# Attention and two mixture layers on one core: k and q in one transfer, half weight tiles side by side in HBM, logits split by half rows

## The chip, the cores and the metric

The kernel runs on one core of one Trainium2 chip. The metric is device time in microseconds, from the first to the last instruction with what lies around them, of one execution of the program. Times are medians over runs; profiles are of one execution.

## What is computed

```python
def _attn_ref(q, k, v):                     # q, k, v: (4, 8, 576, 64) float32
    scores = scale * np.matmul(q, k.transpose(0, 1, 3, 2))
    mask_local = (rel >= 0) & (rel < 32)                        # heads 0 to 3
    mask_strided = (rel >= 0) & (pos[None, :] % 32 == pos[:, None] % 32)   # heads 4 to 7
    ...                                     # softmax over the allowed positions
    return np.matmul(attn, v)

def _moe_ref(x, phi, w1, w2):               # x: (2304, 512); soft mixture, 8 experts, 4 slots each
    logits = x @ phi                        # (2304, 32)
    d = softmax(logits, axis=0); slot_input = d.T @ x
    for e in range(8):
        slot_out[e] = relu(slot_input[e] @ w1[e]) @ w2[e]       # 512 -> 1024 -> 512
    return softmax(logits, axis=1) @ slot_out

def _moe2_ref(x, w_gate, w_val, w_out):     # gated MLP, 512 -> 1536 -> 512
    return (silu(x @ w_gate) * (x @ w_val)) @ w_out
```

A local head attends to the last 32 positions; a strided head attends to every 32nd position before its own. The gate, value and output weights of the last layer come as float64 and are converted on the chip; the rest is float32.

## The kernel before

**Attention.** There are 16 units; a unit is one head of a pair of batches (`bp`), its 64 dimensions of the first batch on partitions 0 to 63 and of the second on 64 to 127. Within each batch pair the order of heads is 0, 1, 4, 5, 2, 3, 6, 7, so units 2, 3, 6, 7, 10, 11, 14, 15 are strided (`y` is 1). For strided heads the host reorders the 576 positions (t, r), t being 0 to 17 and r 0 to 31, so that those with equal r lie together; they are in the order (r, t). A strided head is then local too: both kinds work on nine tiles of 64 positions with a window of 96 keys (local) or 80 keys (strided).

For each unit, `load_qk` brings q and k (one transfer each, 128 rows of 2304 bytes) into one of three buffers, and `load_v` brings v (64 rows of 4680 bytes) into partitions 32 to 95 (local) or 16 to 79 (strided) of one of two buffers; three POOL copies (L261) then repeat the overlap between windows on the partitions below. `qk` makes the scores (L285), with scale, mask and maximum on DVE (L289, L290); `expo` the exponentials on ACT (L295); `tr` transposes on PE (L303) with copies on ACT (L304); `pv` multiplies with v (L320) and divides on DVE.

**The loop** (L590 to L619) runs steps n = 0 to 18, as an order written out by hand. In step n come `qk(n)`, `load_qk(n+3)`, `tr(n-1)`, `expo(n, 0)`, side work, `expo(n, 1)`, `pv(n-1)`, `load_v(n+1)`, and two half weight tiles (`load_half`); then further side work. All these transfers are issued by SP, on one queue, in that order.

**Logits.** Two heads give one tile of x, with 128 features. After each pair of heads `xtr` transposes that tile on PE (L338), ACT copies it (L339), and `logits` (L358) adds its product with phi to the logits of the batch pair in one PSUM bank. The 576 columns of each batch are split over the partitions: `hf` is the half (288 columns), `b` the batch, and the four (hf, b) lie on four groups of 32 partitions. The logits are kept in the plain order of positions (t, r), and half 0 is t from 0 to 8. A local head's x is read in order. A strided head's x is in order (r, t), so it is read with a step of 18 elements and written in order. There are eight such calls, four of them strided, the last two in steps 14 and 17. Then `tok_max`, `tok_exp` (exponentials into `e2`), `e_perm` (the same in order (r, t), on partitions 64 to 127), and `tok_end` (logits into `Lb`); `etr` and `slot` (L423) form the slot inputs.

**Weights.** 32 tiles of expert weights (1 MB each, 16 of w1, 16 of w2) and three tiles of the last layer come as half tiles of 512 KB, 70 in all, in the order of the list `loads`. In HBM a tile is 128 rows of 8192 bytes, and a half takes 4096 bytes out of each row. Fifteen buffers plus three for the tiles of the last layer hold 36 halves during the attention. The other 34 go to memory that the attention frees; the first of these takes a tile of the tag `x`, which is free when the slot matmuls of the first batch pair (`slot(0, 1)`, step 18) have read it. After the expert weights SP issues the first four whole tiles (1 MB) of the remaining weights of the last layer with `load_g` (L656), and the others when a buffer comes free.

**Last stage.** From about 160 us the gated MLP runs on PE (L794, L795, L821), with conversion of weights on ACT and DVE beside it. It is the larger part of the time.

Of the kernel before, what the change touches and what calls it, by code (L numbers as in the profile page):

```python
# [9 lines left out]
F32 = mybir.dt.float32  # L10
F32R = mybir.dt.float32r
I32 = mybir.dt.int32
BF16 = mybir.dt.bfloat16
AF = mybir.ActivationFunctionType
# [3 lines left out]
S = 576  # L18
HD = 64
NT = 9  # L20
PAD = 32
# [20 lines left out]
NQK = 3  # L42
# [29 lines left out]
def bits(a):  # L72
    return a.view(np.int64)
# [12 lines left out]

def layout(q, k, v, moe_phi, moe_w1, moe_w2, moe2_w_gate, moe2_w_val, moe2_w_out):
    pi = perm_index()
    qh = np.empty((16, 2, HD, S), np.float32)
    kh = np.empty((16, 2, HD, S), np.float32)  # L90
    vw = np.ones((16, 64, 2, NT, HD + 1), np.float32)
    for u, (bp, h) in enumerate(UNITS):
        y = h // 4
        o = pi if y else np.arange(S)
        qh[u] = q[2 * bp:2 * bp + 2, h][:, o].transpose(0, 2, 1)
        kh[u] = k[2 * bp:2 * bp + 2, h][:, o].transpose(0, 2, 1)
        vw[u, ..., :HD] = v[2 * bp:2 * bp + 2, h][:, o].reshape(2, NT, 64, HD).transpose(2, 0, 1, 3)
    w1 = moe_w1.reshape(8, 4, 128, 2, 512).transpose(0, 3, 2, 1, 4).reshape(16, 128, 2048)
    w2 = moe_w2.reshape(8, 2, 4, 128, 512).transpose(0, 1, 3, 2, 4).reshape(16, 128, 2048)
    g = bits(moe2_w_gate).reshape(4, 128, 12, 128)  # L100
    a = bits(moe2_w_val).reshape(4, 128, 12, 128)
    wgv = np.stack([g, a], axis=3).transpose(2, 1, 0, 3, 4).reshape(12, 128, 1024)
    wo = bits(moe2_w_out).reshape(6, 2, 128, 512).transpose(0, 2, 1, 3).reshape(6, 128, 1024)
    phi = moe_phi.reshape(4, 128, 32).transpose(1, 0, 2).reshape(128, 128)
    arrs = dict(cst=constants(), phi=phi, qh=qh.reshape(16, 128, S), kh=kh.reshape(16, 128, S),
                vh=vw.reshape(16, 64, -1),
                w1=w1, w2=w2, wgv=wgv, wo=wo)
    return {n: np.ascontiguousarray(x) for n, x in arrs.items()}


@with_exitstack
def build(ctx: ExitStack, tc: tile.TileContext, cst, phi, qh, kh, vh, w1, w2, wgv, wo, out):
    nc = tc.nc
    PE, ACT, DVE, POOL, SP = nc.tensor, nc.scalar, nc.vector, nc.gpsimd, nc.sync

# [8 lines left out]
    lp = es_ld.enter_context(tc.tile_pool(name="ld", bufs=1, side="right"))  # L124
# [11 lines left out]
    Lb = cp.tile([128, S], F32, name="Lb")  # L136
# [2 lines left out]

    qbd, kt, vt = [], [], []  # L140
    for j in range(NQK):
        qbd.append(lp.tile([128, S], F32, name=f"q{j}"))
        kt.append(lp.tile([128, PAD + S], F32, name=f"k{j}"))
    for j in range(NV):
        vt.append(lp.tile([96, 2 * NT * (HD + 1)], F32, name=f"v{j}"))
    col = lp.tile([128, 128], F32, name="col")
# [14 lines left out]
    def load_half(k, pool=wp, bufs=NB):  # L161
        for _ in range(k):
            if wn[0] >= NW:
                return
            j, hf = loads[wn[0]]
            if j in SPEC:
                wt[j, hf] = (ap_.tile([128, 1024], F32, tag="xT", name="wx", bufs=1) if hf and j == SPEC[0] else
                             ap_.tile([128, 1024], F32, tag="x", name="wx", bufs=6))
            elif j == SPLIT:
                wt[j, hf] = ap_.tile([128, 1024], F32, tag="eT", name="wx", bufs=1) if hf else tmp[:, 0:1024]  # L170
            elif hf == 0:
                a = pool.tile([128, 2048], F32, tag="w", name="w", bufs=bufs)
                if j in PRE:
                    gt[j] = a.bitcast(I32)
                wt[j, 0], wt[j, 1] = a[:, 0:1024], a[:, 1024:2048]
            if j in PRE:
                o, i = wt[j, hf].bitcast(I32), (wgv if j[0] == "g" else wo)[j[1]][:, 512 * hf:512 * hf + 512].bitcast(I32)
            else:
                o, i = wt[j, hf], wsrc[j][:, 1024 * hf:1024 * hf + 1024]
            SP.dma_start(out=o, in_=i)  # L180
            wn[0] += 1

# [64 lines left out]
    def load_qk(u):  # L247
        if u >= 16:
            return
        SP.dma_start(out=qbd[u % NQK], in_=qh[u])  # L250
        SP.dma_start(out=kt[u % NQK][:, PAD:], in_=kh[u])

    def load_v(u):
        if u >= 16:
# [89 lines left out]
    def logits(bp, y, st):  # L344
        first, last = (y, st) == (0, 0), (y, st) == (1, 1)
        if first:
            lg[bp] = bank("lg", 1)
        a = xT.pop((bp, y, st))
        for hf in range(2):
            for b in range(2):  # L350
                o = 64 * hf + 32 * b
                if y:
                    rhs = a[:, b, :].rearrange("p (r t) -> p t r", t=18)[:, 9 * hf:9 * hf + 9, :]
                    dst = lg[bp][o:o + 32, 0:288].rearrange("p (t r) -> p t r", r=32)
                else:
                    rhs = a[:, b, 288 * hf:288 * hf + 288]
                    dst = lg[bp][o:o + 32, 0:288]
                PE.matmul(out=dst, lhsT=phi_t[:, 2 * y + st, :], rhs=rhs, start=first, stop=last,  # L358
                          skip_group_check=True)

# [11 lines left out]
    def tok_exp(bp):  # L372
        mh = nmx[bp]
        e2[bp] = ap_.tile([128, S], F32, tag="e2", name="e2", bufs=1)
        s2 = ap_.tile([64, 2], F32, tag="s2", name="s2", bufs=2)
        for hf in range(2):
            h = slice(64 * hf, 64 * hf + 64)
            ACT.activation(out=e2[bp][0:64, 288 * hf:288 * hf + 288], in_=lg[bp][h, 0:288], func=AF.Exp,
                           bias=mh[h, 2:3], scale=1.0, accum_out=s2[:, hf:hf + 1])
        nmx[bp] = mh, s2  # L380

    def e_perm(bp):
        for hf in range(2):
            DVE.tensor_copy(e2[bp][64:128].rearrange("p (r t) -> p r t", t=18)[:, :, 9 * hf:9 * hf + 9],
                            e2[bp][0:64].rearrange("p (t r) -> p r t", r=32)[:, :, 9 * hf:9 * hf + 9])

    def tok_end(bp):
        r = slice(64 * bp, 64 * bp + 64)
        mh, s2 = nmx[bp]
        DVE.tensor_scalar_mul(m_sb[r], mh[0:64, 2:3], -1.0)  # L390
        DVE.tensor_tensor(out=s_sb[:, bp:bp + 1], in0=s2[:, 0:1], in1=s2[:, 1:2], op=ALU.add)
        DVE.tensor_copy(Lb[r, 0:288], lg[bp][0:64, 0:288])
        DVE.tensor_copy(Lb[r, 288:576], lg[bp][64:128, 0:288])

    eT = ap_.tile([128, NT, 2, 2, 32], F32, tag="eT", name="eT", bufs=1)
    WIN = (((0, 4), (4, 8), (8, 10)), WIN1)
# [98 lines left out]
    with tc.manual_schedule():  # L495
# [155 lines left out]
        def load_g(pool, tag, bufs):  # L651
            if gn[0] < len(gsrc):
                kind, j = gsrc[gn[0]]
                t = pool.tile([128, 2048], F32, tag=tag, name=tag, bufs=bufs)
                gt[kind, j] = t.bitcast(I32)
                SP.dma_start(out=gt[kind, j], in_=(wgv if kind == "g" else wo)[j].bitcast(I32))  # L656
                gn[0] += 1

        def c_soft(q):
# [301 lines left out]
                stage(n)  # L961


_NAMES = ['cst', 'phi', 'qh', 'kh', 'vh', 'w1', 'w2', 'wgv', 'wo']


# [15 lines left out]
```

## Time and profile before

| | us |
|---|---|
| median of 3 runs | 368.44 |
| lowest and highest run | 367.56 and 370.82 |
| the profiled execution | 367.68 |
| its span, from the first to the last instruction | 365.9 |
| PE busy | 341.4 |
| DVE busy | 233.2 |
| ACT busy | 193.9 |
| POOL busy | 139.3 |

The profile has the engines PE (matmul), PEld (weight load of PE), DVE, ACT and POOL, and the DMA queue issued by SP (SPq). Times in its rows are microseconds from the start of the span. The DMA share is the mean busy share of the core's 16 DMA engines. Matmuls are pipelined and their ends are modelled, so PE that is busy is not PE at its peak; a matmul in 32-bit floats shows as two instructions. An arrow names what ended an engine's idle time.

### The profile page before, as it was taken

The numbers are of one execution on the slowest core, as the hardware profiler recorded it, in microseconds if no ns is written. First come the engines' busy times: TensorE is split into PE (matmuls) and PEld (weight loads), VectorE is DVE, ScalarE is ACT, GpSimd is POOL, SyncE is SP. The second block draws the span as 40 slices with busy tenths as digits, with TensorE's granted clock in tenths as the row PEclk, the third lists the DMA queues.
The fourth block names the chain that finished last, engine by engine and source line by source line (L and its number), as shares of the span: only waits on it lengthen the run. The fifth ranks groups of instructions, "written<-read, shape, count | busy, mean of one in ns | idle before, by whom it ended". The sixth has DMA issues, their size and how long they took to land.

```text
span 365.9 us, 7445 instructions
## 1 busy us (share of the span) xinstructions
PE 341.4 (93%) x2860; PEld 249.3 (68%) x2860; DVE 233.2 (64%) x487; ACT 193.9 (53%) x462; POOL 139.3 (38%) x147
## 2 busy tenths in 40 slices
PE   8869999899879999979999999999998999999995
PEld 4758677788657333246786668677685788888885
DVE  4957858867744026276987998999787924241442
ACT  2966977787631004146775656556456445344441
POOL 2213222122110020024848497356459564444431
PEclk9989999899999999996999999999999999999999
DMA  7999999998849999982042444333300003030321
GB/s 256 384 298 382 316 315 383 286 372 282 291 151 381 402 407 407 419 338 116 1 134 97 127 186 147 115 116 116 115 0 3 1 0 117 0 115 2 116 104 69
DMA packets 21188, 71.94 MB, mean 197 GB/s; under 512 B 2592, under 2 KB 2976, under 8 KB 19232
## 3 DMA queue, kind: packets, MB, share of 16 engines
q1 hardware_dynamic: 21008, 71.45, 54.8%
q8 instruction: 23, 0.38, 0.4%
q14 instruction: 13, 0.11, 0.1%
q10 hardware_dynamic: 144, 0.01, 0.0%
HBM read 66.73 MB, written 4.72 MB: 195 GB/s over the span
## 4 chain that ended last, share of the span: by engine, by line
PE 59%; DMA 18%; DVE 8%; ACT 5%; POOL 4%; issue 4%; SPq 1%; DVEq 0%; POOLq 0%; ACTq 0%
PE o L821 31%; DMA v<-in_vh 7%; DMA w<-in_w 5%; PE pv L320 4%; PE sc L285 4%; PE tr L303 3%; PE gv L794 3%; DMA g<-in_wgv 3%; DMA wx<-in_w 3%; PE gv L795 3%; PE tr L338 2%; DVE h L801 2%; PE lg L358 2%; PE gv L774 2%; PE sc L626 1%
## 5 line engine op out<-in xcount | busy, mean ns | idle before, releaser
L803 POOL TENSOR_TENSOR hl<-h,hh 128x512 fp32r<-128x512 f32 (+1 forms) x60 | 72.4, 1208 | 90.7 <-ACT hh L802 90.5
L821 PE MATMUL o<-woh,hh 128*128 128x512 f32 (+1 forms) x222 | 86.7, 392 | 0.2 <-DVE acc L846 0.2
L821 PE MATMUL o<-wol,hh 128*128 128x512 f32 (+1 forms) x222 | 86.0, 389 | 0.0
L801 DVE TENSOR_TENSOR h<-gv,sg 128x512 f32<-128x512 f32 (+1 forms) x59 | 37.5, 636 | 55.8 <-ACT sg L800 42.5
L821 PE MATMUL o<-woh,hl 128*128 128x512 f32 (+1 forms) x222 | 66.8, 390 | 0.6 <-POOL hl L803 0.4
L802 ACT CAST hh<-h 128x512 fp32r<-128x512 f32 (+1 forms) x60 | 34.7, 578 | 54.7 <-DVE h L801 54.7
L261 POOL COPY v<-v 32x390 f32<-32x390 f32 (+3 forms) x48 | 22.2, 494 | 71.8 <-DMA v<-in_vh 60.6
L821 PEld LDWEIGHTS o<-woh,hh 128*128 128x128 f32 x222 | 42.2, 190 | 10.0 <-DVE acc L846 0.7
L821 PEld LDWEIGHTS o<-woh,hl 128*128 128x128 f32 x222 | 41.8, 190 | 10.4 <-POOL hl L803 1.9
L821 PEld LDWEIGHTS o<-wol,hh 128*128 128x128 f32 x222 | 42.3, 190 | 8.6
L800 ACT ACTIVATE sg<-gv 128x512 f32<-128x512 f32 (+1 forms) x60 | 33.5, 558 | 20.1 <-PE gv L794 19.3
L295 ACT ACTIVATE tmp<-tmp,mx 128x96 f32<-128x96 f32 (+1 forms) x144 | 39.0, 358 | 8.3 <-DVE mx L290 8.3
L320 PEld LDWEIGHTS pv<-v,tmp 96*64 96x64 f32 (+1 forms) x576 | 20.6, 140 | 13.5 <-ACT tmp L295 7.0
L320 PE MATMUL pv<-v,tmp 96*64 96x65 f32 (+1 forms) x576 | 23.9, 231 | 5.9 <-ACT tmp L295 3.1
L285 PE MATMUL sc<-k,q 64*64 64x96 f32 (+1 forms) x576 | 26.4, 245 | 1.7 <-DVE mx L290 1.1
L794 PE MATMUL gv<-cs,St 128*128 128x512 f32 (+1 forms) x60 | 25.6, 426 | 1.9 <-DVE St L783 1.9
L304 ACT COPY tmp<-tr 96x384 f32<-96x384 f32 (+1 forms) x48 | 19.7, 479 | 12.9 <-PE tr L303 12.9
L285 PEld LDWEIGHTS sc<-k,q 64*64 64x64 f32 x576 | 23.7, 138 | 4.1 <-DVE mx L290 1.2
L765 POOL TENSOR_TENSOR wol<-wo,woh 128x512 fp32r<-128x512 f32 x12 | 15.4, 1299 | 24.0 <-DMA g<-in_wgv 24.0
L795 PE MATMUL gv<-cs,St 128*128 128x512 f32 (+1 forms) x59 | 22.4, 379 | 0.2 <-DVE h L801 0.2
L219 DVE SCALAR_TENSOR_TENSOR cv<-g,cv 128x512 int32<-128x512 int32 x30 | 20.8, 692 | 0.6
L303 PE MATMUL tr<-cst_t,tmp 128*96 128x128 f32 (+1 forms) x144 | 19.4, 278 | 1.5 <-ACT xT L339 1.5
(160 smaller groups left out, 486.5 us busy)
## 6 DMA issues: line engine op xcount, KB each, us to landing
w<-in_w SPq DMA_DIRECT2D x56, 512.0 KB, 9.9
g<-in_wgv SPq DMA_DIRECT2D x10, 1024.0 KB, 4.8
g<-in_wo SPq DMA_DIRECT2D x5, 1024.0 KB, 4.8
v<-in_vh SPq DMA_DIRECT2D x16, 292.5 KB, 7.9
q<-in_qh SPq DMA_DIRECT2D x16, 288.0 KB, 9.3
k<-in_kh SPq DMA_DIRECT2D x16, 288.0 KB, 9.0
out<-osb SPq DMA_DIRECT2D x17, 256.0 KB, 2.0
wx<-in_w SPq DMA_DIRECT2D x7, 512.0 KB, 10.9
```

The costliest lines, as they stand in the source:

```text
L261: POOL.tensor_copy(t4[0:W - 64, :, i0:i1, :], t4[64:W, :, i0 - 1:i1 - 1, :])
L285: PE.matmul(out=ps[h, W * (i - i0):W * (i - i0) + W], lhsT=q[h, 64 * i:64 * i + 64], rhs=k[h, c0:c0 + W], start=True, stop=True, skip_grou ...
L295: ACT.activation(out=e[:, i], in_=e[:, i], func=AF.Exp, scale=1.0, bias=mx[:, i:i + 1])
L303: PE.transpose(ps[0:W, 128 * j:128 * j + 128], e[:, 3 * t + j], ident)
L320: PE.matmul(out=ps[64 * b:64 * b + 64, 65 * (i - i0):65 * (i - i0) + 65], lhsT=attile[0:W, i, 64 * b:64 * b + 64], rhs=v[0:W, 65 * (NT * b ...
L794: PE.matmul(out=pg[:, 0:n], lhsT=St[f][:, 0:128], rhs=csf[:, t0:t0 + n], start=True, stop=True)
L795: PE.matmul(out=pvv[:, 0:n], lhsT=St[f][:, 128:256], rhs=csf[:, t0:t0 + n], start=True, stop=True)
L800: ACT.activation(out=sg[:, 0:n], in_=pg[:, 0:n], func=AF.Silu)
L801: DVE.tensor_tensor(out=h[:, 0:n], in0=pvv[:, 0:n], in1=sg[:, 0:n], op=ALU.mult)
L802: ACT.copy(hh[bi, f][:, 0:n], h[:, 0:n])
L803: POOL.tensor_tensor(out=hl[bi, f][:, 0:n], in0=h[:, 0:n], in1=hh[bi, f][:, 0:n].bitcast(F32), op=ALU.subtract)
L821: PE.matmul(out=o[:, 0:c], lhsT=(a, a, l)[i][:, 128 * t:128 * t + 128], rhs=(woh, wol, woh)[i][f][:, c * k:c * k + c], start=(first and i ...
```

## The change

The host puts k and q of a unit into one array `kq`, k first, and `load_qk` brings both in one transfer into one buffer, in which q now lies behind k. The host stores expert weights and the last layer's weights by half tiles, so that a half tile is one piece of 512 KB; whole tiles (`load_g`) are then read as two rows of 4096 bytes for each partition. The logits are split over the partitions by r rather than by t: half 0 is r from 0 to 15. A strided head's x is then read in order and written to PSUM with a step of 16 elements; a local head's x is read in runs of 16 elements and written in order. `tok_exp`, `e_perm` and `tok_end` follow that split.

```diff
-    qh = np.empty((16, 2, HD, S), np.float32)
-    kh = np.empty((16, 2, HD, S), np.float32)
+    kq = np.empty((16, 2, HD, 2, S), np.float32)
...
-        qh[u] = q[2 * bp:2 * bp + 2, h][:, o].transpose(0, 2, 1)
-        kh[u] = k[2 * bp:2 * bp + 2, h][:, o].transpose(0, 2, 1)
+        kq[u, :, :, 0] = k[2 * bp:2 * bp + 2, h][:, o].transpose(0, 2, 1)
+        kq[u, :, :, 1] = q[2 * bp:2 * bp + 2, h][:, o].transpose(0, 2, 1)
...
+    w1, w2 = (a.reshape(16, 128, 2, 1024).transpose(0, 2, 1, 3) for a in (w1, w2))
+    wgv, wo = (a.reshape(-1, 128, 2, 512).transpose(0, 2, 1, 3) for a in (wgv, wo))
...
-        qbd.append(lp.tile([128, S], F32, name=f"q{j}"))
-        kt.append(lp.tile([128, PAD + S], F32, name=f"k{j}"))
+        a = lp.tile([128, PAD + 2 * S], F32, name=f"k{j}")
+        kt.append(a)
+        qbd.append(a[:, PAD + S:])
...
-                o, i = wt[j, hf].bitcast(I32), (wgv if j[0] == "g" else wo)[j[1]][:, 512 * hf:512 * hf + 512].bitcast(I32)
+                o, i = wt[j, hf].bitcast(I32), (wgv if j[0] == "g" else wo)[j[1], hf].bitcast(I32)
             else:
-                o, i = wt[j, hf], wsrc[j][:, 1024 * hf:1024 * hf + 1024]
+                o, i = wt[j, hf], wsrc[j][hf]
...
-        SP.dma_start(out=qbd[u % NQK], in_=qh[u])
-        SP.dma_start(out=kt[u % NQK][:, PAD:], in_=kh[u])
+        SP.dma_start(out=kt[u % NQK][:, PAD:], in_=kq[u])
...
                 o = 64 * hf + 32 * b
+                dst = lg[bp][o:o + 32, 0:288]
                 if y:
-                    rhs = a[:, b, :].rearrange("p (r t) -> p t r", t=18)[:, 9 * hf:9 * hf + 9, :]
-                    dst = lg[bp][o:o + 32, 0:288].rearrange("p (t r) -> p t r", r=32)
+                    rhs = a[:, b, 288 * hf:288 * hf + 288]
+                    dst = dst.rearrange("p (t r) -> p r t", r=16)
                 else:
-                    rhs = a[:, b, 288 * hf:288 * hf + 288]
-                    dst = lg[bp][o:o + 32, 0:288]
+                    rhs = a[:, b, :].rearrange("p (t r) -> p t r", r=32)[:, :, 16 * hf:16 * hf + 16]
+                    dst = dst.rearrange("p (t r) -> p t r", r=16)
...
-            ACT.activation(out=e2[bp][0:64, 288 * hf:288 * hf + 288], in_=lg[bp][h, 0:288], func=AF.Exp,
+            ACT.activation(out=e2[bp][0:64].rearrange("p (t r) -> p t r", r=32)[:, :, 16 * hf:16 * hf + 16],
+                           in_=lg[bp][h, 0:288].rearrange("p (t r) -> p t r", r=16), func=AF.Exp,
...
-            DVE.tensor_copy(e2[bp][64:128].rearrange("p (r t) -> p r t", t=18)[:, :, 9 * hf:9 * hf + 9],
-                            e2[bp][0:64].rearrange("p (t r) -> p r t", r=32)[:, :, 9 * hf:9 * hf + 9])
+            DVE.tensor_copy(e2[bp][64:128, 288 * hf:288 * hf + 288].rearrange("p (r t) -> p r t", t=18),
+                            e2[bp][0:64].rearrange("p (t r) -> p r t", r=32)[:, 16 * hf:16 * hf + 16])
...
-        DVE.tensor_copy(Lb[r, 0:288], lg[bp][0:64, 0:288])
-        DVE.tensor_copy(Lb[r, 288:576], lg[bp][64:128, 0:288])
+        for hf in range(2):
+            DVE.tensor_copy(Lb[r].rearrange("p (t r) -> p t r", r=32)[:, :, 16 * hf:16 * hf + 16],
+                            lg[bp][64 * hf:64 * hf + 64, 0:288].rearrange("p (t r) -> p t r", r=16))
...
-                SP.dma_start(out=gt[kind, j], in_=(wgv if kind == "g" else wo)[j].bitcast(I32))
+                SP.dma_start(out=gt[kind, j].rearrange("p (h c) -> p h c", h=2),
+                             in_=(wgv if kind == "g" else wo)[j].rearrange("h p c -> p h c").bitcast(I32))
```

## Rows read from the trace of the kernel before

**Rows 1.** Stretches: length, busy us of each engine, granted PE clock, DMA share, GB/s

```profile
2.00:4.00 2.00, 2.00 (x6) 0.64 (x5) 0.10 (x1) 0.45 (x1) 0.00 (x0) 1.00 0.85 287
4.00:6.00 2.00, 2.00 (x20) 1.05 (x20) 1.23 (x5) 0.00 (x0) 0.09 (x1) 1.00 0.93 305
...
24.00:30.00 6.00, 6.00 (x70) 5.29 (x74) 3.97 (x11) 2.06 (x5) 0.81 (x3) 0.72 1.02 282
30.00:39.40 9.40, 9.40 (x177) 7.86 (x173) 7.80 (x20) 8.00 (x27) 3.26 (x7) 1.00 1.04 408
39.40:46.50 7.10, 6.39 (x113) 4.50 (x114) 4.94 (x13) 6.22 (x21) 2.05 (x5) 1.00 1.04 291
46.50:53.00 6.50, 6.02 (x98) 4.69 (x92) 4.37 (x11) 5.22 (x17) 1.01 (x4) 1.00 1.03 273
53.00:62.50 9.50, 9.47 (x165) 8.04 (x167) 8.04 (x21) 6.79 (x23) 2.71 (x7) 1.00 1.04 410
62.50:69.00 6.50, 4.81 (x95) 3.54 (x89) 4.89 (x15) 4.67 (x17) 1.01 (x3) 1.00 1.03 278
69.00:75.00 6.00, 6.00 (x86) 5.48 (x85) 5.09 (x16) 4.46 (x15) 0.77 (x3) 0.72 1.04 283
...
130.00:140.00 10.00, 9.66 (x84) 4.25 (x80) 3.87 (x12) 1.62 (x3) 2.02 (x1) 1.00 1.03 410
...
154.00:162.50 8.50, 7.89 (x53) 3.74 (x50) 4.41 (x10) 4.03 (x10) 2.51 (x2) 1.00 1.01 419
```

**Rows 2.** POOL timeline, copies of v of units 6, 7, 10, 11: start, us, what

```profile
45.33 1.31 POOL L261 COPY v<-v 16x260 f32<-16x260 f32 x3 [5.05 <-DMA v<-in_vh]
52.13 1.31 POOL L261 COPY v<-v 16x260 f32<-16x260 f32 x3 [5.49 <-DMA v<-in_vh]
...
68.35 1.31 POOL L261 COPY v<-v 16x260 f32<-16x260 f32 x3 [5.49 <-DMA v<-in_vh]
74.89 1.31 POOL L261 COPY v<-v 16x260 f32<-16x260 f32 x3 [5.23 <-DMA v<-in_vh]
```

**Rows 3.** PE timeline, attention: PV (L320), transposes of x (L338), logits (L358), slots (L423)

```profile
52.12 1.95 PE L320 MATMUL pv<-v,tmp 80*64 80x65 f32 x36 [0.36 <-ACT tmp L295]
...
68.81 2.04 PE L320 MATMUL pv<-v,tmp 80*64 80x65 f32 x36 [1.69 <-ACT tmp L304]
70.78 2.13 PE L338 MATMUL tr<-cst_t,x 128*128 128x128 f32 x9
...
75.58 0.69 PE L358 MATMUL lg<-xT,phi_t 128*32 128x288 f32 x8
77.87 1.22 PE L320 MATMUL pv<-v,tmp 80*64 80x65 f32 x36
...
85.01 1.20 PE L338 MATMUL tr<-cst_t,x 128*128 128x128 f32 x9
...
88.65 1.27 PE L358 MATMUL lg<-xT,phi_t 128*32 128x288 f32 x8
...
103.76 1.26 PE L358 MATMUL lg<-xT,phi_t 128*32 128x288 f32 x8 [0.73 <-ACT xT L339]
104.95 2.19 PE L423 MATMUL tr<-x,eT 128*64 128x128 f32 x36
```

**Rows 4.** Chain that ended last, in order of time: start, us, what

```profile
107.19 0.30 SPq L180
...
135.93 10.16 DMA w<-in_w
...
146.15 10.96 DMA g<-in_wgv
...
318.48 2.72 PE o L821 x12
```

**Rows 5.** Waits of the DMA queue: who waited for whom, us in total, times, longest

```profile
SPq L250 <- DMA v<-in_vh: 7.3, 9, 1.1
```

**Rows 6.** DMA issues: what, how many, KB each, median us to landing

```profile
g<-in_wgv SPq DMA_DIRECT2D x10, 1024.0 KB, 4.8
```

More of the change, by code (lines that the diff above doesn't have):

```diff
@@ L103, in layout @@
     wo = bits(moe2_w_out).reshape(6, 2, 128, 512).transpose(0, 2, 1, 3).reshape(6, 128, 1024)
+    w1, w2 = (a.reshape(16, 128, 2, 1024).transpose(0, 2, 1, 3) for a in (w1, w2))
+    wgv, wo = (a.reshape(-1, 128, 2, 512).transpose(0, 2, 1, 3) for a in (wgv, wo))
     phi = moe_phi.reshape(4, 128, 32).transpose(1, 0, 2).reshape(128, 128)
-    arrs = dict(cst=constants(), phi=phi, qh=qh.reshape(16, 128, S), kh=kh.reshape(16, 128, S),
+    arrs = dict(cst=constants(), phi=phi, kq=kq.reshape(16, 128, 2 * S),
                 vh=vw.reshape(16, 64, -1),
@@ L111, in build @@
 @with_exitstack
-def build(ctx: ExitStack, tc: tile.TileContext, cst, phi, qh, kh, vh, w1, w2, wgv, wo, out):
+def build(ctx: ExitStack, tc: tile.TileContext, cst, phi, kq, vh, w1, w2, wgv, wo, out):
     nc = tc.nc
@@ L961, in build @@
                 stage(n)
-_NAMES = ['cst', 'phi', 'qh', 'kh', 'vh', 'w1', 'w2', 'wgv', 'wo']
+_NAMES = ['cst', 'phi', 'kq', 'vh', 'w1', 'w2', 'wgv', 'wo']
 def kernel(**inputs):
```

## The prediction

> **What bounds the kernel now.** I read the busy time of the engines in stretches first, then the POOL timeline (each copy there starts when a v load has landed), the PE timeline, the chain of waits, and the DMA queue's waits and issues. Step n runs scores of unit n, transposes and PV of unit n-1; an operand with a number, as v(10), belongs to that unit.
>
> Up to about 69 us the DMA engines are the limit: their share is 1.02 or more in every stretch from 24 to 69, while PE has holes [rows 1]. PV waits for its v: v(6) lands at 45.33 and v(7) at 52.13, and PV of unit 7 starts at 52.12, beside the first copy of its v [rows 2, 3]. v(10) lands at 68.35; PV of unit 10 starts at 68.81 [rows 2, 3].
>
> The rate is not even. It is 408 and 410 GB/s in 30 to 39.4 and 53 to 62.5, but 291 in 39.4 to 46.5 and 278 in 62.5 to 69 [rows 1]. The slow stretches follow the loads of v of strided units (2, 3, 6, 7, 10, 11 and so on), which go to partitions 16 to 79, where those of local units go to 32 to 95.
>
> From 69 us to 107 us the limit is PE with the ACT and DVE work that feeds it: v(11) lands at 74.89 and its copies need 1.31 us, so it could be used at 76.2, and PV of unit 11 starts at 77.87 [rows 2, 3]. The stage ends with logits at 103.76 and the slot matmuls at 104.95 [rows 3]; only their end frees the `x` tile that the next weight half needs, and the chain goes through the DMA queue at 107.19 [rows 4]. After that transfers are the limit again up to the last expert weights, at 410 GB/s [rows 1], with the chain through two DMA steps, one of weights and one of the first gate tile, until 157.1 [rows 4]. The rest is the gated MLP on PE, which the change leaves as it is, apart from loads that are hidden. So a microsecond counts in full if it is saved on transfers before 69 us, on PE's path between 69 and 107 us, or on transfers between 107 and 157 us. Saved elsewhere it counts for nothing.
>
> **The change part by part.**
>
> *k and q in one transfer.* Per unit one issue and one semaphore write go, and each partition's two rows of 2304 bytes become one of 4608. The price of a row: half tiles (4096 bytes) move at 410 GB/s in 130 to 140, whole tiles (8192 bytes) at 419 in 154 to 162.5 [rows 1]. With 16 engines a row then takes 4096 / (410/16) = 159.8 ns and 8192 / (419/16) = 312.8 ns, so one row more costs at most 2 x 159.8 - 312.8 = 6.8 ns, the semaphore writes in it. Each engine has 8 rows fewer per unit: 8 x 6.8 = 54 ns. Ahead of v(10) in the queue lie the k and q of 13 units (0 to 12): 13 x 54 = 0.7 us. The lower end is 0, if the whole difference comes from the holes, below.
>
> At the start the engines are not yet full: share 0.85 in 2 to 4 and 0.93 in 4 to 6, against 1.03 later [rows 1]. That is (0.18 + 0.10) x 2 / 1.03 = 0.54 us of idle time between small transfers. With one transfer for two, v(0) and all behind it are issued one issue earlier. I take 0.3 us, between 0 and 0.54.
>
> The order of the queue stays k and q, v, w, w. What shifts is how far SP runs ahead. SP waits for transfers to land before it issues new ones, as L250 for a v load 9 times, 7.3 us in all [rows 5]; the distance between the two is 8 transfers, 1.6 steps so far and 2 steps after. More bytes can then be queued ahead of v(n+1). But its place in the order doesn't move, and where the engines are full, landing is set by the bytes ahead. I cost this at 0; the cover is the full DMA share.
>
> *Half tiles without holes.* Half tiles keep their 4096-byte rows, but the rows now lie side by side in HBM. With holes they already move at 410 GB/s; whole tiles without holes at 419 [rows 1]. So removing the holes gains at least 0 and at most 2.1%: of the 34 half tiles (17.8 MB, 43.5 us) issued after 107 us at most 0.9 us, of the some 22 (11.5 MB, 28 us) ahead of v(10) at most 0.6 us. I take 0: a row's fixed cost explains the same 2%, and the two can't both be counted. The gate and output tiles of the last stage pay in return: two rows of 4096 in place of one of 8192. The four that are queued behind the weights move 4.2 MB, 10.0 us at 419 and 10.2 at 410 GB/s. The first of these ends a step of the chain, and the others are waited for later, so 0.05 to 0.2 us; I take 0.1 lost. The others land 4.8 us after issue [rows 6], long before their turn, and are hidden.
>
> *Logits.* A local call takes 0.69 us, a strided one 1.27 and 1.26 [rows 3]. Local calls read SBUF in order; strided ones read every 18th element and write PSUM in order. After, strided calls read in order and write every 16th element, and local calls read runs of 16 elements and write in order. Local calls I leave at 0.69: runs of 64 bytes are nearer to the row read in order than to the row read one element at a time. Of the four strided calls the first two, in steps 6 and 10, lie ahead of waits for v and gain nothing. The last two, at 88.65 and 103.76, lie on PE's path and gain 0.58 and 0.57 if the stepped write is free, together 1.15 us. No row shows a matmul with a stepped PSUM write. The near end is that row of 0.69, the far end the stepped read's 1.27. I take the near end: in the MLP twelve matmuls write 512 columns each in 2.72 us [rows 4], 2720 / 6144 = 0.44 ns a column, while here a partition is written 2 x 288 times (each matmul shows as two, each partition belongs to one of four) in 0.69 us, 1.2 ns a column. The write side is asked less than half as often as it has been seen to answer, and has room for a slower write.
>
> By the Trainium skill, "PSUM — Partial Sum Buffer", section "Specifications (TRN2)", PSUM has 8-byte lines and any non-contiguous access pattern slows matmuls significantly. No run here shows it; by that rule the 1.15 us drop out of the sum, or turn into a loss.
>
> *The copies around the logits.* The two exponentials, the two permuting copies and the two copies to `Lb` per batch pair keep their counts and sizes; only their steps change, in runs of 16 elements or whole rows. I cost them at 0. They are issued 0.6 us earlier with the logits.
>
> **Sum.** 0.7 + 0.3 - 0.1 + 1.15 = 2.05 us. The profiled execution took 367.68 us with a span of 365.9; it becomes 365.6. The median of the runs, 368.44, is 0.76 above the profiled one, so I forecast 366.4.
>
> **Rivals.**
>
> *The stepped write costs what the stepped read cost.* Strided calls stay at 1.27 us. Left are 0.9 us: 367.5. For it: reading with steps doubled the time [rows 3]. Against it: the pace argument above.
>
> *The stepped write costs more.* Both calls on the path get slower. At twice the strided call of now, 2.5 us, they add 2 x 1.25 = 2.5 us, less 0.9: 370.0, slower than before. It turns the sign at 1.27 + 0.9/2 = 1.72 us for a call.
>
> *The clock stays up.* After the wait for v(10) PE ran at a granted clock of 0.72 in 69 to 75 [rows 1], the lower of the two levels, 1.2 GHz, in part of it: PV of unit 10 took 2.04 us against 1.22 at 2.4 GHz for unit 11, and the transposes of x 2.13 against 1.20 [rows 3]. That is 1.7 us on PE's path. v(10) 1 us earlier shortens the wait; if it becomes too short for the fall, the time is 364.7. Against it: the stretch before has 4.81 us of work in 6.5 [rows 1], and most of the wait remains.
>
> *The holes make the slow stretches.* Then these go at 408. Of 24 to 30, 39.4 to 53 and 62.5 to 69, at 273 to 291 GB/s [rows 1], about 30% of 26 us is lost time, some 8 us ahead of v(10); PE's own work would hold back part of it, and some 6 us would be left: 360.4. Against it: the same holes move at 410 GB/s after 107 us [rows 1], and in 30 to 39.4 too. By the Trainium skill, "SBUF — State Buffer", section "Door 1: The DMA port swizzle", partitions 32 apart share a port; then 16 to 79 load some ports twice and 32 to 95 none, and the slow stretches, which the change does not touch, stay: the sum stands at 366.4 rather than 360.4.
>
> *The deeper queue holds back v.* If more bytes get ahead of v in real order, as through engines of different pace, v(10) comes one k and q transfer (0.6 MB, 1.5 us) later, and the gain of 1.0 us turns into a loss of 0.5: 367.9.
>
> **How the numbers follow.** Chances: forecast 0.40; stepped write as dear as the read 0.20; dearer 0.10; clock 0.12; holes 0.08; deeper queue 0.10. About 1% (3.7 us) is what a measurement of this kernel can tell from no change. Faster by over 1% (under 364.8) are the holes' case, the clock's case for the larger part, and a tenth of the forecast with the holes' 1.5 us on top: 0.08 + 0.09 + 0.05 = 0.22. Slower by over 1% (over 372.1) would need a stepped write of over 3.5 us a call or two losses at once: 0.08. Within 1%: 0.70. The range leaves out the holes' case and the dearer half of the dear write: 363.0 to 369.6. The forecast's own range is 364.9 (with the holes' 1.5 us) to 367.4 (rows and start at 0).
>
> **What would show it.** In the profile after: one issue of 576 KB per unit; strided calls of L358's successor at about 0.69 us and local ones unchanged; v(10) landing about 1 us earlier; the rate in the stretches of strided v loads still below 300 GB/s; weights at 410 to 419 GB/s after the attention; the slot matmuls' end, and the restart of the weights, near 105 us and not 107.1. A strided call above 1.7 us, a rate in the slow stretches near 400, or a v that lands later than now would make the prediction wrong.

## The result and the profile after

| | before | after |
|---|---|---|
| median of 6 runs, us | 368.91 | 364.76 |
| lowest and highest run, us | 367.56, 370.82 | 362.70, 368.71 |
| the profiled execution, us | 367.68 | 362.70 |
| its span, us | 365.9 | 360.9 |
| mean granted clock in it | 0.981 | 0.991 |

The ratio of the times is 0.987, with an interval of 0.982 to 0.992: 1.3% faster. Medians here are over all runs, while ratios leave out slow runs, those more than 1.5% above the fastest of their kernel. The median lies 1.6 us under the forecast of 366.4 and inside the range. The whole change was then measured three times more beside the experiments. Over all 36 runs of it the median is 365.51 us, against 368.58 over the 75 runs of the kernel before that were made with them: 3.1 us. One execution of a kernel differs from the next by up to 7 us and more (362.7 to 369.6 for the whole change), so a single profile shows what each piece costs, but not when it comes in a typical execution.

Stretches of the profiled execution after: length, then busy us of PE, PEld, DVE, ACT and POOL with counts, granted clock, DMA share, GB/s.

```profile
28.00:37.50 9.50, 9.50 (x178) 7.96 (x178) 8.49 (x21) 8.10 (x27) 3.26 (x7) 1.00 1.03 410
37.50:43.40 5.90, 4.79 (x95) 3.75 (x95) 4.91 (x13) 5.61 (x19) 0.89 (x3) 1.00 1.03 295
43.40:49.60 6.20, 6.08 (x98) 4.87 (x98) 4.13 (x11) 4.53 (x14) 1.32 (x4) 1.00 1.03 304
49.60:58.70 9.10, 9.10 (x169) 7.81 (x166) 7.25 (x20) 7.35 (x25) 2.54 (x6) 1.00 1.02 411
58.70:65.00 6.30, 5.46 (x97) 4.22 (x95) 5.26 (x16) 4.79 (x16) 1.31 (x4) 1.00 1.03 316
65.00:71.20 6.20, 5.65 (x98) 4.82 (x98) 5.81 (x17) 6.10 (x19) 1.34 (x4) 1.00 1.04 312
134.00:144.00 10.00, 10.00 (x93) 3.12 (x89) 5.69 (x17) 4.70 (x7) 0.00 (x0) 1.00 1.03 408
148.00:157.00 9.00, 8.14 (x54) 3.61 (x53) 4.11 (x9) 3.86 (x9) 2.51 (x2) 1.00 1.03 410
```

The picture of [rows 1] is still there: fast stretches at 410, slow stretches at 295 to 316 where v of strided units is loaded, and 408 after the attention, now without holes. What is new is the granted clock of 1.00 in 65 to 71.2, where before had 0.72 after its wait for v(10).

POOL timeline after, the copies of v(1), v(6), v(7), v(10) and v(11): start, length, what, idle time before and what ended it.

```profile
11.24 1.37 POOL L262 COPY v<-v 32x260 f32<-32x260 f32 x3 [4.50 <-DMA v<-in_vh]
...
43.35 1.30 POOL L262 COPY v<-v 16x260 f32<-16x260 f32 x3 [5.01 <-DMA v<-in_vh]
49.53 1.31 POOL L262 COPY v<-v 16x260 f32<-16x260 f32 x3 [4.88 <-DMA v<-in_vh]
...
65.00 1.30 POOL L262 COPY v<-v 16x260 f32<-16x260 f32 x3 [4.97 <-DMA v<-in_vh]
71.16 1.31 POOL L262 COPY v<-v 16x260 f32<-16x260 f32 x3 [4.86 <-DMA v<-in_vh]
```

In this execution v(10) lands 3.35 us earlier than in [rows 2]. PE timeline after:

```profile
65.55 1.42 PE L321 MATMUL pv<-v,tmp 80*64 80x65 f32 x36 [1.39 <-ACT tmp L305]
66.90 1.20 PE L339 MATMUL tr<-cst_t,x 128*128 128x128 f32 x9
70.77 0.69 PE L360 MATMUL lg<-xT,phi_t 128*32 128x288 f32 x8
...
83.92 0.69 PE L360 MATMUL lg<-xT,phi_t 128*32 128x288 f32 x8
...
98.42 1.06 PE L360 MATMUL lg<-xT,phi_t 128*32 128x288 f32 x8 [0.35 <-ACT xT L340]
99.41 2.19 PE L427 MATMUL tr<-x,eT 128*64 128x128 f32 x36
```

Beside [rows 3] three things stand out. The strided call at 83.92 takes 0.69 us, as a local one does (70.77); before it took 1.27. The last one shows 1.06, but it waits for the last copy of xT in the middle of its matmuls. And PV of unit 10 and the transposes of x behind it run at 1.42 and 1.20 us, where before had 2.04 and 2.13. The slot matmuls start at 99.41 rather than 104.95.

That last number settles the end. In the thirteen profiled executions of this study these matmuls start between 98.2 and 107.5 us, and the span ends 259.9 to 261.5 us later in every one (before 365.9 - 104.95 = 260.95; after 360.9 - 99.41 = 261.5). Nearly all of what moves the time happens in the attention, up to these matmuls.

### The profile page after: what moved, and what is told of

Its sections match the earlier page's. It is cut to its first block, busy times and chain, and to the rows that moved or that the text cites. A ratio compares the mean times of both kernels' runs of the same rounds, so it can differ in the third digit from the quotient of the medians.

```text
span 360.9 us, 7431 instructions
## 1 busy us (share of the span) xinstructions
PE 338.2 (94%) x2860; PEld 246.2 (68%) x2860; DVE 235.8 (65%) x487; ACT 193.5 (54%) x462; POOL 139.8 (39%) x147
## 4 chain that ended last, share of the span: by engine, by line
PE 63%; DVE 11%; DMA 8%; ACT 6%; POOL 6%; issue 4%; DVEq 0%; POOLq 0%; ACTq 0%; SPq 0%
PE o L826 31%; PE pv L321 4%; PE sc L286 4%; PE gv L799 3%; DMA g<-in_wgv 3%; DMA wx<-in_w 3%; PE tr L304 3%; PE pv L719 3%; PE gv L800 2%; DMA v<-in_vh 2%; POOL hl L808 2%; POOL wol L770 2%; DVE h L806 2%; ACT tmp L296 2%; PE sc L630 2%
## 5 line engine op out<-in xcount | busy, mean ns | idle before, releaser
L286 PE MATMUL sc<-k 64*64 64x96 f32 (+1 forms) x576 | 26.1, 239 | 1.8 <-DVE tmp L290 1.6
L286 PEld LDWEIGHTS sc<-k 64*64 64x64 f32 x576 | 22.8, 133 | 4.9 <-DVE tmp L290 2.1
L321 PE MATMUL pv<-v,tmp 96*64 96x65 f32 (+1 forms) x576 | 22.7, 227 | 3.5 <-ACT tmp L305 2.2
L321 PEld LDWEIGHTS pv<-v,tmp 96*64 96x64 f32 (+1 forms) x576 | 19.8, 137 | 8.9 <-ACT tmp L305 7.6
```

The lines of the kernel that those rows point to most:

```text
L286: PE.matmul(out=ps[h, W * (i - i0):W * (i - i0) + W], lhsT=q[h, 64 * i:64 * i + 64], rhs=k[h, c0:c0 + W], start=True, stop=True, skip_grou ...
L321: PE.matmul(out=ps[64 * b:64 * b + 64, 65 * (i - i0):65 * (i - i0) + 65], lhsT=attile[0:W, i, 64 * b:64 * b + 64], rhs=v[0:W, 65 * (NT * b ...
```

## The experiments

**One part alone, and the whole again.** Each kernel is the one before with one part of the diff, all else as it was: k and q in one transfer; half tiles side by side; logits split by half rows.

```diff
# only k and q: before, and
...
+        SP.dma_start(out=kt[u % NQK][:, PAD:], in_=kq[u])
# only half tiles: before, and
...
+                o, i = wt[j, hf], wsrc[j][hf]
...
# only logits: before, and
...
+                    rhs = a[:, b, 288 * hf:288 * hf + 288]
+                    dst = dst.rearrange("p (t r) -> p r t", r=16)
...
```

> The kernel before with one part of the change: k and q of a unit in one transfer. Theory A (the terms of the forecast, and the rest of the gain from the clock): 0.7 to 1.3 us faster than before, v(10) lands 1 us earlier (67.3), the slow stretches stay at 273 to 291 GB/s. Theory B (one large transfer in place of two small ones is what raised the slow stretches to 295 to 316 GB/s): 2 to 3 us faster, v(10) near 65.5, slow stretches near 305 GB/s. Theory C (the holes did that): as A, and less than 1 us.

> The kernel before with one part of the change: weight tiles stored by halves. Theory A: 0 to 0.5 us faster, slow stretches at 273 to 291 GB/s, v(10) at 68. Theory B: the same as A. Theory C (holes in HBM make the slow stretches slower): 1.5 to 3 us faster, slow stretches above 300 GB/s, v(10) near 66.5.

> The kernel before with one part of the change: logits split by r. All theories: calls of 0.69 us for local and strided heads. Theory A: the two late strided calls are on PE's path, 1.1 to 1.6 us faster, with nothing gained before v(10), which stays at 68.35 within 0.3. Rival D (the logits of steps 6 and 10 also free the buffer of v earlier, so that transfers are issued earlier): 2 us or more, v(10) 0.5 us earlier or more.

> The whole change again, on the same chip as the three parts. If the parts add up, its gain is the sum of the three. Theory A with the clock: its profile either has no stretch of low granted clock in the attention (then about 5 us faster in the profile) or has one or two (then 1.7 us less for one that lies behind v(10)); the median over runs 3.5 to 4.5 us faster, with more spread than a sum of fixed terms would have.

| 12 runs each, before on the same chip 368.48 | median us | ratio and interval |
|---|---|---|
| only k and q | 367.56 | 0.9993 (0.996 to 1.003) |
| only half tiles | 368.29 | 0.998 (0.993 to 1.002) |
| only logits | 366.68 | 0.995 (0.992 to 0.999) |
| whole change | 365.50 | 0.994 (0.990 to 0.997) |

The logits alone are the only part whose interval leaves out 1. The differences of the medians are 0.9, 0.2 and 1.8 us, together 2.9, and the whole gives 3.0; by the ratios they are 0.3, 0.8 and 1.7 us, together 2.8, and the whole gives 2.3. Each is uncertain by 1.3 to 1.6 us. The parts add up within that; how the first two share their 1.1 us is not shown, and the whole gives less than the 3.5 to 4.5 us that was expected.

Theories B and C, by which a part raises the slow stretches, are not borne out. In the five steps that end with the landing of v(3), v(6), v(7), v(10) and v(11), each counted from the landing of the v before, the rate is 291 to 316 GB/s with k and q alone, 290 to 307 with half tiles alone and 281 to 311 with the logits alone, which touch no transfer; before it was 279 to 293. The five steps took no less time, 34.3, 34.5 and 34.5 us together against 33.7 before, and v(10) landed at 67.75, 68.53 and 68.73, not near 65.5 or 66.5.

The pieces themselves are read more sharply than the totals. The kernel with the logits alone, PE timeline:

```profile
89.10 0.69 PE L359 MATMUL lg<-xT,phi_t 128*32 128x288 f32 x8
...
104.99 1.06 PE L359 MATMUL lg<-xT,phi_t 128*32 128x288 f32 x8 [0.35 <-ACT xT L339]
```

The calls are as short as in the whole change, so this edit alone does it. What they give to PE's path can be read from the start of PV of unit 11 to the start of the last slot matmuls: 27.08 us before [rows 3], and in the kernel with k and q alone (first pair of lines) 27.09; with the whole change, third time (second pair), 25.91:

```profile
77.38 1.22 PE L319 MATMUL pv<-v,tmp 80*64 80x65 f32 x36
...
104.47 2.19 PE L422 MATMUL tr<-x,eT 128*64 128x128 f32 x36
```

```profile
78.32 1.22 PE L321 MATMUL pv<-v,tmp 80*64 80x65 f32 x36
...
104.23 2.19 PE L427 MATMUL tr<-x,eT 128*64 128x128 f32 x36
```

The kernel with half tiles alone has 27.09 too, and the two other repeats of the whole change 25.89 and 25.91: the logits are worth 1.2 us there, whatever the execution did before. (With the logits alone it is 27.65, as the granted clock falls to 0.50 from 98 us on, inside that stretch.)

Whole tiles in the stretch that ends the weights, with k and q alone (whole tiles as before), then with half tiles alone:

```profile
152.00:160.00 8.00, 7.56 (x54) 2.97 (x48) 2.68 (x7) 3.23 (x8) 2.51 (x2) 1.00 1.02 421
```

```profile
134.00:144.00 10.00, 9.66 (x84) 4.29 (x82) 5.53 (x18) 2.68 (x5) 1.01 (x1) 1.00 1.03 410
152.00:160.00 8.00, 7.55 (x55) 2.89 (x47) 2.53 (x7) 1.55 (x4) 1.85 (x2) 1.00 1.03 410
```

Half tiles without holes move at 410 GB/s, as with holes [rows 1], and whole tiles read as two rows fall from 421 to 410. Holes are worth nothing; the length of a row is. In the last line the edit leaves the transfer and its bytes as they are and cuts each row of 8192 bytes in two; by the prediction's formula the added row costs 2 x 159.8 - 311.3 = 8.3 ns, somewhat more than the 6.8 of the prediction.

**k and q in other pieces.** From the whole change: four rows of 1152 bytes for each partition in one transfer (24 rows more for each engine and unit; the host stores `kq` to match), then two transfers as before, from the merged array.

```diff
...
-        SP.dma_start(out=kt[u % NQK][:, PAD:], in_=kq[u])
# rows of 1152
+        SP.dma_start(out=kt[u % NQK][:, PAD:].rearrange("p (h c) -> p h c", h=4),
+                     in_=kq[u].rearrange("h p c -> p h c"))
# two transfers
+        SP.dma_start(out=qbd[u % NQK], in_=kq[u][:, S:])
+        SP.dma_start(out=kt[u % NQK][:, PAD:PAD + S], in_=kq[u][:, 0:S])
```

> The changed kernel, k and q still in one transfer, but stored in HBM in four pieces, so that each partition has four rows of 1152 bytes in place of one of 4608. By the forecast's price of 6.8 ns a row, 24 rows more for each engine and unit cost 0.16 us a unit: v(10) lands 2.1 us later than in the changed kernel, the fast stretches fall from 410 to about 397 GB/s, and the time grows by 1 to 2 us. If a row costs nothing in this kernel: no change of either.

> The changed kernel with q and k brought by two transfers out of the merged array, rows of 2304 bytes with holes: issues, rows and the distance of 8 transfers are as before the change, the rest as after. By the forecast: 0.7 to 1.3 us slower than the changed kernel. If merging is worth nothing: the same within 0.5 us, and still 1.5 to 2 us faster than the kernel before through the logits.

> The changed kernel on the same chip as the three above. If its first measurement owed part of its 4 us to fewer drops of the granted clock, it is again about 2 us faster than before, with runs of 363 to 369 us, and the runs with a higher mean clock are the shorter ones: 1.0 to 1.3 us for each 0.005 of mean clock.

| 12 runs each, before on the same chip 368.48 | median us | ratio and interval |
|---|---|---|
| rows of 1152 | 367.39 | 0.998 (0.993 to 1.002) |
| two transfers | 367.76 | 1.000 (0.996 to 1.004) |
| whole change again | 366.23 | 0.995 (0.991 to 0.999) |

The fast stretches with rows of 1152, to be set beside 410 and 411 of the whole change:

```profile
30.00:37.00 7.00, 6.99 (x132) 6.05 (x130) 6.11 (x17) 4.50 (x16) 1.42 (x4) 1.00 1.04 403
...
53.00:61.00 8.00, 7.93 (x153) 6.90 (x151) 6.29 (x19) 6.88 (x25) 2.25 (x6) 1.00 1.04 403
```

A unit moves 0.59 MB of k and q, 0.30 of v and 1.05 of weights, 1.94 MB. At 410 GB/s that takes 4.73 us, at 403 it takes 4.81: 82 ns for 24 rows, 3.4 ns a row, half of the 6.8 that the prediction used (the fast stretches of the whole change lie between 408 and 411, which makes 2.5 to 4 ns). The time from the landing of v(7) to that of v(9), 9.39 us here and 9.13 to 9.19 in the four profiles of the whole change, makes 4 to 5 ns. The total of this run (1.2 us over the whole change of the same chip, where 24 rows x 13 units x 3.4 ns = 1.1) fits, but is uncertain by more than its size. Two transfers cost 1.5 us against one, a little over the expected 0.7 to 1.3. That is more than what merging gave alone (0.9 us by the medians, 0.3 by the ratio), but each difference is uncertain by 1.3 us or more, and both contain the forecast of 1.0 (0.7 + 0.3).

**Where v is put.** From one landing of v to the next, the slow stretches stood at 260 to 324 GB/s in every profile so far, with and without holes. The rivals for their cause were the holes, which the half tiles have now cleared, and the partitions to which v of strided units goes. First the windows of strided heads are made 96 wide, as for local heads, so that their v goes to partitions 32 to 95 too; PE, DVE and ACT work on 96 keys in place of 80. This is done once on top of the whole change, once on the kernel before.

```diff
-WID = (96, 80)
-SHIFT = (0, 16)
+WID = (96, 96)
+SHIFT = (0, 0)
...
-        c[:, 6 + i] = (64 * i + q) // 18 * 18 - 64 * i + 16
+        c[:, 6 + i] = (64 * i + q) // 18 * 18 - 64 * i + 32
...
-    ms = lp.tile([128, 9, 80], BF16, name="ms")
+    ms = lp.tile([128, 9, 96], BF16, name="ms")
...
-            low(80, 5)
+            low(96, 4)
...
-                cut(ms[:, i], 6 + i, ALU.is_lt, h[:, 0:80])
+                cut(ms[:, i], 6 + i, ALU.is_lt, h)
```

Then the destination alone is moved, with windows of 80 as they were. This kernel leaves out the matching shift of the rows that PV reads, so its strided heads multiply with the wrong rows of v; it serves for the time alone:

```diff
-        SP.dma_start(out=t[W - 64:W], in_=vh[u])
+        SP.dma_start(out=t[32:96], in_=vh[u])
```

> The changed kernel with windows of 96 keys for strided heads too, so that their v is loaded to partitions 32 to 95 like that of local heads; each strided unit pays for it with 16 more masked columns (scores 1.70 in place of 1.46 us, exponentials 2.50 in place of 2.38). Theory P (the slow stretches come from v on partitions 16 to 79): every stretch from 8 to 80 us moves 390 to 412 GB/s, v(10) lands before 62 us, no wait for v stays long, and the whole takes 3 to 6 us less than the changed kernel. Rival (the slow stretches have to do with the work or the data of strided units, or with chance): rates of 270 to 320 GB/s remain, and the time is 0 to 2 us longer for the wider windows.

> The kernel before, with windows of 96 keys for strided heads and so their v on partitions 32 to 95, none of the change. The transfers no longer limit the attention, so what the change is worth then comes from the late logits on PE's path alone: the same kernel with the change took 359.9 us, this one should take 361.0 to 362.0 by the forecast's price of 1.15 us for the logits and 0 for transfers. If the merged transfers still gain their 1 us, 362.5 to 363.5. Rival (the wide windows help only together with the merged transfers): 366 or more.

> The changed kernel with the v load of strided units sent to partitions 32 to 95 as for local units, and nothing else: windows stay at 80 keys, so strided heads multiply with the wrong rows of v. It separates the place of v from the wider windows. Theory P: the rate is 390 to 412 GB/s in all stretches, v(10) lands at 57 to 60 us, and the time is that of the wide windows or up to 1.5 us less. Rival (the wider windows changed the order of work, and that took the slow stretches away): slow stretches of 270 to 320 GB/s remain and the time is near 366.

> The changed kernel once more, on the same chip as the two above: 2.0 to 2.9 us faster than before, slow stretches at 280 to 320 GB/s, one to three drops of the granted clock ahead of 100 us in its profile.

| 6 runs each | median us | before, same chip | ratio and interval |
|---|---|---|---|
| whole change, windows of 96 | 359.92 | 368.48 | 0.979 (0.974 to 0.984) |
| before, windows of 96 | 362.45 | 369.46 | 0.982 (0.977 to 0.987) |
| whole change, v to 32 to 95, windows of 80 | 358.58 | 369.46 | 0.970 (0.966 to 0.975) |
| whole change, third time | 364.76 | 369.46 | 0.987 (0.983 to 0.992) |

The same stretches of the whole change, third time, and with only the destination of v moved:

```profile
30.00:37.00 7.00, 7.00 (x134) 6.16 (x130) 6.47 (x17) 5.27 (x19) 1.31 (x3) 1.00 1.02 408
37.00:45.00 8.00, 5.96 (x110) 4.65 (x105) 5.79 (x14) 7.76 (x26) 1.78 (x5) 1.00 1.03 304
45.00:53.00 8.00, 7.30 (x120) 5.78 (x122) 4.41 (x12) 5.55 (x17) 2.16 (x5) 1.00 1.03 303
...
61.00:69.00 8.00, 6.31 (x118) 5.11 (x118) 6.77 (x18) 6.74 (x23) 2.30 (x6) 0.94 1.04 289
```

```profile
30.00:37.00 7.00, 6.81 (x132) 6.06 (x128) 6.55 (x17) 5.60 (x20) 2.58 (x6) 1.00 1.01 374
37.00:45.00 8.00, 7.88 (x142) 6.52 (x143) 6.63 (x18) 7.43 (x25) 1.31 (x3) 1.00 1.01 396
45.00:53.00 8.00, 8.00 (x149) 6.69 (x148) 6.94 (x17) 7.02 (x22) 3.11 (x6) 1.00 1.01 384
...
61.00:69.00 8.00, 5.99 (x78) 5.27 (x78) 7.30 (x21) 6.46 (x20) 2.27 (x6) 0.79 1.02 401
```

Sixty-four rows of 4680 bytes, put 16 partitions higher, lift the rate of everything in the queue from about 300 to 384 to 401 GB/s, with bytes, rows and order unchanged. (Two stretches stay under the 390 GB/s that was expected of all.) Its v(10), against the third run of the whole change:

```profile
60.64 1.31 POOL L262 COPY v<-v 16x260 f32<-16x260 f32 x3 [2.79 <-DMA v<-in_vh]
```

```profile
67.40 1.31 POOL L262 COPY v<-v 16x260 f32<-16x260 f32 x3 [5.42 <-DMA v<-in_vh]
```

It lands 6.8 us earlier (at 60.64, where 57 to 60 was expected), and the time falls by 364.76 - 358.58 = 6.2 us. That is the loss which the prediction put at some 6 us, in its rival on the holes. The destination causes it: shown, since no other instruction and no other transfer was changed. The Trainium skill, "SBUF — State Buffer", section "Door 1: The DMA port swizzle", says why this may be: within the lower 64 partitions, and within the upper 64, those 32 apart share a port, so 16 to 31 and 48 to 63 meet on the same ports while others get nothing, and 32 to 95 spread evenly. The traces agree as to which destination is slow; no run here looks at ports, and no other place of the 64 rows was run, so a start at 16 as such is a rival that stays.

With windows of 96 v(10) lands at 58.68 on top of the change and at 60.98 without it, and the stretches of the first read:

```profile
37.00:45.00 8.00, 8.00 (x164) 7.09 (x158) 6.74 (x19) 7.68 (x25) 1.90 (x6) 1.00 1.02 402
45.00:53.00 8.00, 8.00 (x151) 6.67 (x146) 7.40 (x16) 6.62 (x21) 2.47 (x5) 1.00 1.01 397
```

PE is busy throughout these two stretches: where v comes in time, PE's own work is the limit. On the chip where the whole change took 366.23 us, windows of 96 took 359.92, 6.3 us less, beside the 6.2 of the destination alone; what the wider windows cost can't be told from this, as the two differences come from two chips and each is uncertain by some 2 us. With these windows the kernel beats the one before by 2.1% and the whole change by 1.7%.

The two kernels with windows of 96 also price the change where the slow stretches are gone: 2.5 us by their medians, 0.3% or 1.1 us by their ratios to before, since they ran on two chips. The first lies at the edge of the two forecasts (361.0 to 362.0 without a gain from merging, 362.5 to 363.5 with it) and doesn't decide between them; the rival of 366 or more is out. From PV of unit 11 to the slot matmuls the change saves 1.29 us here (27.74 against 26.45), so the gain of the logits is left; whether one of transfers is, stays open.

The third time the whole change gained 4.7 us, more than the 2.0 to 2.9 that was expected; its profile has one fall of the granted clock ahead of 100 us.

## Why the prediction was right, point by point

*Logits: right.* Forecast 1.15 us for two calls on PE's path, at 0.69 us each with a stepped PSUM write that costs nothing. The call at 83.92 fell by 1.27 - 0.69 = 0.58. The last one shows 1.06, but its end counts: it comes 0.73 us after the last copy of xT is done and came 1.30 after before, 0.57 less. Both agree to 0.01 us, and together they make the 1.2 us between PV of unit 11 and the slots in the runs above. In the profiled execution 0.35 us of it is given back ahead of the last PV, where the transposes wait 1.89 us for ACT; they waited 1.54 before and 1.54 or 1.55 in the three other profiles of the whole change, so this belongs to the execution. The part alone gave 1.8 us by the medians (0.3 to 3.1 by its interval), which holds 1.15. The rule that the prediction weighed against this (any non-contiguous pattern slows matmuls significantly, the Trainium skill, "PSUM — Partial Sum Buffer", section "Specifications (TRN2)") doesn't hold for this write: a step of 16 elements, 64 bytes, cost 0.00 of 0.69 us. That is at this call's 1.2 ns a column; no faster call with such a write was run. Both rivals on the stepped write, 0.30 together, are out.

*A row's price: right for weights, too high for k and q.* The prediction gave all of the difference between 410 and 419 GB/s to rows, 6.8 ns a row. For weight tiles the runs bear that out: without holes half tiles stay at 410, and whole tiles cut into two rows fall to 410. The run with 24 more rows of k and q gave 3.4 ns. For 13 units that makes 13 x 8 x 3.4 = 0.35 us, not 0.7 (up to 0.5 by the landings of v). The step that failed was to carry the price of a row from weight tiles to the shorter rows of k and q. Why it is lower there stays open, and that rows of 2304 bytes cost as little as those of 1152 is assumed.

*The start: too low.* The prediction took 0.3 us, between 0 and 0.54. v(1) lands at 11.24 after, 11.82 before. In the eight profiled executions with one transfer it lands at 11.56 in the mean (11.24 to 11.94), in the five with two at 12.26 (11.82 to 12.64): 0.7 us, over the upper bound. The first v itself is not earlier (5.3 to 7.0 against 5.6 to 7.4), so the gain is made behind it, between 6 and 12 us. The copies of v(1) in the kernel with k and q in one transfer, alone:

```profile
11.64 1.30 POOL L260 COPY v<-v 32x260 f32<-32x260 f32 x3 [3.62 <-DMA v<-in_vh]
```

The two errors cancel, which is luck: 0.35 + 0.7 is the 1.0 that was forecast for merging, if the 0.7 lasts up to v(10). The full DMA share between the two speaks for that; no run isolates it.

*Half tiles: right.* Forecast 0 for the holes and 0.1 us lost on whole tiles. The rates are 408 to 410 without holes against 410 with, and 410 against 419 to 421 for whole tiles; alone the part measures 0.2 us by the medians and 0.8 by the ratio, with an interval that holds 0. A loss of 0.1 us is too small for any run here to show. The rival that had the holes make the slow stretches is out: they stay near 300 GB/s without holes.

*The queue of SP: right.* The waits moved, as the prediction said they might. Waits of the DMA queue before, for the load of v: who waited for whom, us in total, times, longest; then those after, and the issues of k and q.

```profile
SPq L258 <- PE pv L320: 14.3, 6, 3.6
...
SPq L258 <- DMA w<-in_w: 7.0, 5, 1.8
```

```profile
SPq L259 <- PE pv L321: 40.8, 14, 4.3
...
SPq L252 <- DMA k<-in_kq: 2.6, 5, 1.0
...
k<-in_kq SPq DMA_DIRECT2D x16, 576.0 KB, 9.5
```

The load of v (L258, L259 after) now waits for PE to free its buffer, 14 times, and no longer for a weight half to land; the load of k and q waits for transfers for 2.6 us, where it waited for 7.3 [rows 5]. The load of v is issued with enough bytes ahead of it that the DMA share stays at 1.02 or more. The rival of the deeper queue shows no sign: with one transfer v(10) lands at 67.9 us in the mean of five profiles (four of the whole change, one of k and q alone), with two at 69.1 in the mean of four.

*v(10) one microsecond earlier: not to be read from a profile.* It lands at 65.00 here, but at 67.40, 68.86 and 70.65 in the three other profiled executions of the same kernel, against 68.35 before. What the change gives there is some 1 us under a spread of 5.7. Most of what sets whole executions apart lies in the slow stretches: the five steps that end with v(3), v(6), v(7), v(10) and v(11) took 31.7 us together here and 34.1, 35.2 and 38.0 in the others, whose runs took 362.70, 366.49, 367.79 and 369.62 us. So 2.4, 3.5 and 6.3 us of the 3.8, 5.1 and 6.9 between them lie in these steps.

*The clock: in the profiled execution the rival came true.* PE waited 1.39 us ahead of PV of unit 10 there, against 1.69 before [rows 3], the granted clock stayed at 1.00, and PV and transposes behind it took 1.42 + 1.20 us in place of 2.04 + 2.13: 1.55 us, as the 1.7 of that rival. In the three other profiles of the whole change it did not: PE waited 1.69 to 3.69 us, the clock fell to the lower level (in the third run of the whole change in 68.0 to 74.8), and PV took 2.34 to 2.48 us and the transposes 2.18. The third run's lines:

```profile
67.54 2.34 PE L321 MATMUL pv<-v,tmp 80*64 80x65 f32 x36 [1.69 <-ACT tmp L305]
69.81 2.18 PE L339 MATMUL tr<-cst_t,x 128*128 128x128 f32 x9
```

So it is a matter of the execution, and the profile after is a lucky one. On average the clock shifts a little: the mean granted clock over 36 runs of the whole change is 0.983, over 75 of before 0.980. Within kernels a run is 0.22 to 0.26 us shorter per 0.001 of mean clock (one fit over all kernels, without and with the longest runs), so 0.003 goes with 0.7 to 0.8 us. At equal clock by that fit, the whole change gains 2.2 us, uncertain by 0.5; the sum was 2.05. The first six runs had a mean clock of 0.985; against 0.980 that goes with 1.1 to 1.4 us, most of the rest of their 4.15 us. That the clock brings these 0.7 to 0.8 us, rather than both following from shorter waits in the slow stretches, is argued and not shown.

*The profiled execution, step by step.* Its slots start 5.54 us before [rows 3]: 3.35 at v(10), 1.55 by the clock, 1.15 by the logits, less 0.35 of the wait for ACT, make 5.7. After the weights 5.16 are left (the last expert matmul starts at 149.91, before at 155.07). What took the 0.4 us is not shown: the weights move at 408 to 410 GB/s in both. The span keeps 5.0. The chain goes through the same kinds of steps as in [rows 4], one of weights and one of the first gate tile:

```profile
112.75 10.08 DMA wx<-in_w
...
140.97 10.96 DMA g<-in_wgv
```

Of the 5.0 us by which this span is shorter, 2 belong to the change by the sum, and the rest to an execution without a fall of the clock in the attention and with faster slow stretches (295 to 316 GB/s, where before had 273 to 291). That is why the sum must be held against many runs.

## What to carry to other kernels

Price a layout change by its parts with the nearest row of the trace, and then ask which part of the queue is slow and why: here all three parts of the change were worth 2 to 3 us, and the 6 us lay in the one transfer that the change left as it was, whose destination partitions slowed everything queued with it. A rate that falls whenever one kind of transfer is under way is a hint at that transfer's destination, and moving the destination alone is a one-line experiment. When runs of one kernel differ by 2%, take enough of them, put the granted clock beside each time, and use single profiles for the price of an instruction, not for when it happens.

## What the runs showed of the hardware that was not expected

- A load of 64 rows of 4680 bytes to partitions 16 to 79 drops the rate of all queued transfers from about 410 GB/s to 260 to 324 for most of a step (from landing to landing, in all ten profiles with v there); to 32 to 95 it stays at 367 to 413 up to v(10) (three profiles). Price here: 6.2 of 365 us.
- An fp32 matmul that writes PSUM with a step of 16 elements takes the same 0.69 us as one that writes in order, while one that reads SBUF with a step of 18 elements and writes in order took 1.27; reading SBUF in runs of 16 elements costs nothing (0.69).
- Half tiles picked out of rows of 8192 bytes in HBM move as fast as half tiles side by side: 410 and 410 GB/s.
- Cutting rows costs time even at a full DMA share: each row more costs 3.4 to 5 ns of an engine where a row of 4608 bytes becomes four of 1152 (410 against 403 GB/s), and about 8 ns where one of 8192 becomes two of 4096 (421 against 410).
- Executions of one kernel differ by up to 7 us; in the four profiles of the whole change most of that lies in the steps that load v to partitions 16 to 79 (31.7 to 38.0 us for the five).
